# Attention with sorted blocks and a feed-forward layer on one core: query of batch 0 by turning products, weights in column halves, and a new written order

## The chip, the cores and the metric

The kernel runs on 1 core of one Trainium2 chip. The metric is the device time of one execution in microseconds (us). The core has five engines that each work through a queue of their own: TensorE (PE in the profile; its weight loads are PEld), VectorE (DVE), ScalarE (ACT), GpSimd (POOL) and SyncE (SP). PE writes to the accumulators (PSUM) only, and DVE and ACT bring results from there to the on-chip memory. Transfers run on 16 DMA engines. POOL issues the loads that turn float32 into bfloat16 on the way (queue q0 in the profile); SP issues the transposing transfers and the stores (q1).

## What is computed

Shapes: q, k and v are 4 batches x 8 heads x 768 tokens x 64, each head in 8 blocks of 96 tokens; sort_net is 4 x 8 x 8 x 8.

```python
for _ in range(5):                                   # sinkhorn on sort_net
    P = exp(P - max(P, -1)); P /= sum(P, -1) + 1e-9; P /= sum(P, -2) + 1e-9
k_sorted, v_sorted = P mixes the 8 blocks of k, of v  # einsum 'bhij,bhjcd->bhicd'
scores = q_b @ k_sb.T / 8                             # 96 x 96, one block with its own sorted block
attn = softmax(scores);  x = attn @ v_sb              # heads joined: 3072 tokens x 512
h = x @ w_in                                          # 512 -> 2048
g = max(h, 0) + alpha * min(h, 0)
out = g @ w_out                                       # 2048 -> 512, float32
```

## The kernel before, in words

**Work units.** A group g (0 to 31) is one block of one batch over all 8 heads; groups 0 to 7 are batch 0. `attention` makes for each group: scores (s1, 8 products into psS), their row maximum on DVE (tile nm or nf), the exponential on ACT, the weighted sum with v (PV, 8 products into psO), reciprocal `rec` and scaling `xq` on DVE, and the turn of xq into the feature-major tile xT. Batch 0 does not turn its probabilities: a second set of products with the roles exchanged (s2, 16 products, L765 and L756) gives the scores turned, with the maximum subtracted by products. Groups 0 to 15 turn xq by 4 products on PE (L823) and a copy; later groups by an SP transfer.

**Preparation of a batch.** `prep_q` (batch 0 only) brings q in feature-major order into QTz; q's DMA for batch 0 lands in the part of hT that is not yet used. `prep_k` mixes the blocks of k by products with BDK or BDM (matrices that `spread0` and `spread` make from the sinkhorn result) into KT. `conv_v` reorders v, and `prep_v` mixes it into VS. For batch 0 there are 6 units of q, 6 of k, 8 of v; each is some products and one copy out of PSUM (L400 is the helper that all copies share). Batches 1 to 3 have q loaded into QN and turned by SP (`turn_q`), k first spread into KSz by POOL (`conv_k`), v into VDz.

**Feed-forward.** `ffn1` makes, for one of 16 slices ft of 128 hidden features and one chunk of tokens, 4 products into psH (or psP), then ACT writes relu(-h) to t1 (L857) and DVE adds (1-alpha)*t1 to h and stores hT (L860). The chunks are groups (0,2), (2,4) of 192 tokens, then 7 chunks of 4 groups (384 tokens). `ffn2` makes a tile of 128 output tokens in four parts of 4 products each (part p uses ft 4p to 4p+3), copies it to outstg and stores it. The last tile, 23, comes in two halves of columns.

**What sets the order.** Every step is entered by `G.add` with the tiles it reads and writes; the steps are numbered in the order of these calls. `SEQ` is a written list of these numbers: each engine executes its steps in the order in which they stand there, and waits where a step's inputs are not ready. Nothing overtakes: a step that waits holds all later ones of its engine, and POOL's and SP's DMA issues stand in the same queues as their other work. A letter after a number picks the engine (p, a, d) where more are allowed; without it the first allowed one is meant, ACT for `EITHER`. `i15Y` means 15 filler products (L1017, 128 x 512, results not used) into an accumulator named by the letter. `burst` (L912) is a series of tiny products at the start. The planner in `_Graph.arrange` only gives each step a place in the waits; it does not reorder.

**Names used below.** hT<-in_q_dram is batch 0's q, VST<-in_v_dram is v, KS<-in_k_dram is k. VD (in hT) is the reordered v of batch 0. QTz, KT and VS are the prepared q, k and v. The four w_in loads and the two w_out loads are issued by POOL (L931, L936): w_in by 128 rows of 2048 columns each, w_out by halves of its 2048 rows. FFN1 waits for all four parts of w_in.

Of the kernel before, what the change touches and what calls it, by code (L numbers as in the profile page):

```python
# [7 lines left out]
AP = bass.AP  # L8
ACTF = mybir.ActivationFunctionType
# [18 lines left out]
BURST = 110  # L28
# [4 lines left out]
0 2 11 7 3 4 1 8 9 i15Y 22 42 28 14 43 44 45 46 19 47 18 48 5 49 50 51 15 39 52 53 54 6 55 56 57 25 58 29 59  # L33
23 60 61 12 62 63 64 132 65 66 37 31 67 89 68 83 32 69 81 13 70 84 87 71 91 10 88 85 i8Y 72 40 73 90 130 74 75
86 76 133 41 77 82 78 131 92 79 i2Y 134 80 93 138 102 94d i2Y 103 26 104 147 95 105 100 148 96d 98 i4Y 99 24
101d 38 35 111a 113 97d 17 107d i2Y 158 149 106a 108d 21 159 146 i2Y 114 118 115 116 135 160 119 144 109a 124
143 125d 117 150 110a i3Y 136 145 112a i2Y 122 141 120 161 121d 30 20 123 140 36 i3Y 128 126 129d 142 151 127
137 16 139 162 152 163 164 i3G 153 165 154 183 155 166 184 i1P 167 156 157 33 i2Y 185 168 34 169 192 186 195
170 198 193 171 204 174 194 205 201 187 202 196 206 203 199 188 200 219 197 207 216 27 189 213 220 237 217 221
214 190 218 228 191 215 225 238 208 226 222 209 223 227 239 229 210 246 234 224 240 211 247 230 231 212d 235  # L40
260 253 236 290 261 241 232 248 250 242 272 262 251 249 233 291 269 252 254 270 263 350 172 255 243 292 264
271 256 258 265 293 244 312d 278 311 273 279 259d 303 337 280 266 257 245d 284 338 267 281 300 285 294 268 339
299 286 282 310 402 283 313 295 301 296 401 340 287 274 302d 304 288 314 289 347 297 309 305 315 316 298d 319
306d 317 346 341 320 378 318 307 321 322 342 308 379 325 275 323 351 324 177 343 348 326 328 175 380 327 329
355 179 349d 344 331 330 276 352 176 345d 334 381 178 353d 372 332 335 333 382 356 336 360 383 357 389 363 384
373 361 364 354 362 390 365 387 366 388d 393 385 369 367 359 386d 391 368 358 418 392 428 419 370 403 374 429
371 445 420 395 431 396d 375 430 394d 397 376 434 449 452 432 435 377 404 421 448 453 398d 436 405 447 454 181
433 399 444 458 400d 464 437 459 455 465 450 456 406 460 180 479 466 457 482 446 451d 422 182 461 423 478 483
424 476 462 407 484 467 475 477 463 494 408 474 480 495 485 481 425 504 548 486 426d 496 487 509 506 438 507d
491 505 439 488 440 492 497 535 510 493 489 524 511 441 490 515 508 442 525 512 516 534 536 517 513 468 549  # L50
414 526 469 470 521 412 514 471 537d 518 417 522 527 472d 538 523 410 519 498 560 539 499 520 545 411 409 500
542 277 546 413 561 501 540 543 550 416 502 544 562 547 415 554 541d 557 570 551 555 571 563 558 556 572 574
552 596 559 578 573 575 597 528 607 579 605 529 581 598 427 606d 608 590 530 576 580 443 591 577 582 609 583
531 625 599 637 532 584 626 610 636 564 585 587 611 569 565 627 566 634 612 592 586 635d 567 613 588 628 638
589 614 593 568 615 553 616 639d 594 503 619 617 600 620 640 601 595 661 618 641 473 621 622 602 658 623 603
676 659 645 604d 662 677 643 663 642 624 678 644 629 667 630 631 664 668 660 703 669 665 670 704 666 673 671
533 173 691 674 705 675 692 672 688 713 632 685 706 689 633d 690 712 693 686 679 687 700 717 718 701 697 714
702 694 698 715 699 723 695 748 719d 720 696 724 716 738 721 749 739 732 750 647 725 648 733 740 722 649 753
680 646 754d 729 747 681 726 741 682 730 767 776 731 727 707 734 768 683 781 735 728 769 777 708 709 778 755
751 736d 758 756 770 812 802 757 759 787 760 752 710 761 803 780 764 762 788 846 763 765 804 657 766 789 779d  # L60
651 793 653 742 805 794 782 743 784 744 654 790 795 785 745 656 783 786 771 837 791 772 650 813 773 796 838
655 774 799 797 814 825 652 798 800 792 811 815 839 801 826 816d 847 822 853 819 823 840 849 872 824 820 806
848 817 821 827 711 818 873 831 807 834 808 832 828 833 835 874 836 850 854 829d 883 857 851d 882 866 855 875
852 858 856 841 859 880 900 684 881 842 860 901 884 861 863 843 910 746 885 867 862 864 887 902 865 908 886
844 888 909d 911 891 868 889 903 892 912 893 876 913 869 809 877 890 878 914 897 915 737 894 870 879 898 934
# [10 lines left out]
1147 1142 1138 1143 1144 1151 1148 1152 1139 1153 1149 1150 1157 1140d 1220 1158 1154 1141 1159 1181 1155 1156  # L76
# [234 lines left out]
def bass_sinkhorn_attn__then__act_prelu_kernel(  # L311
# [610 lines left out]
    for u in range(6):  # L922
        prep_q(u, -50, (BANK_H + BANK_O + BANK_S)[u])
# [136 lines left out]
```

## Time and profile before

| what | value |
|---|---|
| median of 3 runs | 237.89 us (237.42 to 238.29) |
| the profiled execution | 238.1 us, of which span 236.4 us |
| PE busy | 227.3 us (96% of the span), 2483 products |
| DVE, ACT, POOL busy | 167.4, 158.7, 99.0 us |
| granted TensorE clock | 1.0 in all 40 slices |
| moved by DMA | 31.36 MB, mean 133 GB/s |

The span runs from the first to the last instruction. The 1.7 us between span and time lie outside of what the profile shows. The duration of a product includes the time in which its result drains (about 0.17 us) beside the next one, so the start of one product to the start of the next is what it costs PE; a busy PE is not PE at its peak. In the timeline, a line is a start, a duration, the engine, the line of code, the operation, destination<-sources, shapes and a count of merged instructions.

### The profile page before, as it was taken

What the parts mean: (1) busy time and instruction counts of PE and PEld (TensorE: products, weight loads), DVE (VectorE), ACT (ScalarE), POOL (GpSimd) and SP (SyncE); (2) the same over time, 40 slices, a digit from 0 to 9 for tenths busy, and PEclk for the clock granted to TensorE, in tenths of its full rate; (3) what the DMA queues carried; (4) which work ended last, traced back from release to release, by engine and by line L of the source; (5) the groups of instructions that cost most, each with busy time, mean ns of one, the idle gap of its engine ahead of it and who ended that gap; (6) DMA issues with size and microseconds to landing.
All of it is one profiled execution on the core that took longest, in us unless ns stands there. A gap on an engine that the chain in (4) does not pass through costs nothing.

```text
span 236.4 us, 6202 instructions
## 1 busy us (share of the span) xinstructions
PE 227.3 (96%) x2483; PEld 141.6 (60%) x2513; DVE 167.4 (71%) x343; ACT 158.7 (67%) x429; POOL 99.0 (42%) x144
## 2 busy tenths in 40 slices
PE   7898989999999999999999999999999999999995
PEld 3455677777666756655656565556555555555553
DVE  4764789998899988776888777566777667554420
ACT  4579456688989898676767778777676783543332
POOL 7989507934679995308999534000000000000000
PEclk9999999999999999999999999999999999999999
DMA  5999999995697998998889967594445222310023
GB/s 96 212 207 214 169 219 197 179 190 120 115 181 137 85 210 137 185 183 179 147 133 113 167 70 150 131 145 104 94 137 131 63 50 50 137 42 2 0 101 124
DMA packets 71981, 31.36 MB, mean 133 GB/s; under 512 B 64512, under 2 KB 67344, under 8 KB 71952
## 3 DMA queue, kind: packets, MB, share of 16 engines
q0 software_dynamic: 23408, 13.63, 44.3%
q1 hardware_dynamic: 48544, 17.33, 36.2%
q8 instruction: 20, 0.33, 0.6%
q14 instruction: 9, 0.07, 0.1%
HBM read 27.28 MB, written 6.29 MB: 142 GB/s over the span
## 4 chain that ended last, share of the span: by engine, by line
PE 85%; DMA 5%; ACT 4%; DVE 2%; POOL 2%; issue 2%; POOLq 0%
PE psH L847 34%; PE psYP L886 30%; DMA VST<-in_v_dram 5%; PE psS L886 4%; PE psS L741 4%; PE psO L797 3%; PE psYP L698 2%; PE psYP L657 2%; ACT hT L400 2%; PE psS L756 2%; PE psS L765 1%; PE psO L823 1%; ACT VS L400 1%; POOL VDz L484 1%; DVE nm L750 1%
## 5 line engine op out<-in xcount | busy, mean ns | idle before, releaser
L860 DVE SCALAR_TENSOR_TENSOR hT<-t,omaT,psH 128x384 bf16<-128x384 f32 (+1 forms) x139 | 77.3, 570 | 35.6 <-ACT t L857 34.4
L847 PE MATMUL psH<-xT,w_in_bf 128*128 128x384 bf16 (+1 forms) x556 | 97.9, 310 | 0.5 <-DVE rec L805 0.5
L857 ACT ACTIVATE t<-psH 128x384 f32<-128x384 f32 (+1 forms) x139 | 62.6, 462 | 41.9 <-PE psH L847 39.1
L886 PE MATMUL psYP<-w_out_bf,hT 128*128 128x512 bf16 x308 | 78.6, 379 | 1.6 <-issue 0.2
L847 PEld LDWEIGHTS psH<-xT,w_in_bf 128*128 128x128 bf16 x556 | 49.1, 98 | 29.3 <-DVE hT L860 2.3
L886 PEld LDWEIGHTS psYP<-w_out_bf,hT 128*128 128x128 bf16 x336 | 31.4, 98 | 29.7 <-ACT outstg L400 0.2
L777 ACT ACTIVATE Esb<-psS,nf 96x96 bf16<-96x96 f32 x192 | 46.2, 344 | 4.0 <-DVE nf L750 4.0
L400 POOL COPY VDz<-VST 64x384 bf16<-64x384 bf16 x40 | 33.9, 847 | 20.0 <-PE psYP L698 9.8
L644 POOL COPY KSz<-KS 64x512 bf16<-64x512 bf16 x36 | 22.1, 615 | 18.2 <-DMA KS<-in_k_dram 9.2
L750 DVE TENSOR_REDUCE nf<-psS 96x8 f32<-96x768 f32 x24 | 22.8, 951 | 4.1 <-PE psS L741 3.6
L808 DVE TENSOR_TENSOR xq<-psO,rec 96x512 bf16<-96x512 f32 x31 | 21.3, 688 | 0.7
L429 POOL DMA_DIRECT2D QN<-in_q_dram x24 | 19.8, 858 | 0.3 <-POOL QN L489 0.3
L400 ACT ACTIVATE outstg<-psYP 128x512 f32<-128x512 f32 x18 | 10.8, 598 | 5.3 <-PE psYP L886 5.1
L1017 PE MATMUL psYP<-identb 128*128 128x512 bf16 x46 | 13.3, 420 | 0.7 <-ACT identb L400 0.7
L797 PEld LDWEIGHTS psO<-VS,ET 112*128 112x128 bf16 x248 | 11.0, 98 | 3.4 <-ACT ET L788 0.3
L741 PEld LDWEIGHTS psS<-KT,QTz 128*96 128x96 bf16 x192 | 11.5, 125 | 2.1 <-ACT Esb L777 0.2
L797 PE MATMUL psO<-VS,ET 112*128 112x65 bf16 x248 | 12.7, 194 | 0.0
L741 PE MATMUL psS<-KT,QTz 128*96 128x96 bf16 x192 | 12.6, 208 | 0.0
L400 DVE CAST VS<-psYP 112x512 bf16<-112x512 f32 x15 | 10.3, 689 | 3.0 <-PE psYP L703 2.1
L698 PEld LDWEIGHTS psYP<-BDV,VDz 128*128 128x128 bf16 x192 | 8.3, 98 | 3.1 <-DVE VS L400 0.3
L805 DVE RECIPROCAL rec<-psO 96x8 f32<-96x8 f32 x31 | 6.2, 201 | 5.3 <-PE psO L797 5.2
L698 PE MATMUL psYP<-BDV,VDz 128*128 128x64 bf16 x192 | 9.5, 193 | 0.0
(139 smaller groups left out, 201.5 us busy)
## 6 DMA issues: line engine op xcount, KB each, us to landing
out_dram<-outstg SPq DMA_DIRECT2D x23, 256.0 KB, 2.4
KS<-in_k_dram POOLq DMA_DIRECT2D x3, 768.0 KB, 7.7
QN<-in_q_dram POOLq DMA_DIRECT2D x24, 96.0 KB, 6.0
w_in_bf<-in_moe_w_in_dram POOLq DMA_DIRECT2D x4, 512.0 KB, 11.2
w_out_bf<-in_moe_w_out_dram POOLq DMA_DIRECT2D x2, 1024.0 KB, 23.3
VST<-in_v_dram POOLq DMA_DIRECT2D x4, 384.0 KB, 16.0
hT<-in_q_dram POOLq DMA_DIRECT2D x1, 768.0 KB, 7.0
VST<-in_v_dram POOLq DMA_DIRECT2D x1, 768.0 KB, 10.7
```

The lines of the kernel that those rows point to most:

```text
L400: return e.activation(o, i, ACTF.Copy) if e is nc.scalar else e.tensor_copy(o, i)
L644: G.add(POOL, lambda e, hp=hp: e.tensor_copy(AP(KSz, hp * 64 * 3072 + u % 3 * 1024 + hp * 64, [[3072, 64], [128, 8], [1, 64]]), AP(KS[n], ...
L698: inst = e.matmul(AP(t, off + dd * 64, [[row, 128], [1, 64]]), AP(VDz, (u % VSL * 8 + dd) * 128, [[VSL * 1024, 128], [1, 128]]), AP(BDV, b ...
L741: inst = e.matmul(o, AP(QTz[n], hp * 3072 + h4 * 768 + i * 96, [[6144, 128], [1, 96]]), AP(KT[n], (h4 * 8 + i) * bk, [[ld, 128], [64, 2], ...
L750: G.add(DVE, lambda e: e.tensor_reduce(AP(nx, 0, [[8, 96], [4, 2], [1, 4]]), AP(psX, 0, [[1024, 96], [512, 2], [96, 4], [1, 96]]), AxisLis ...
L777: inst = e.activation(AP(Esb[me], p * 128, [[1024, 96], [64, 2], [1, 48]]), AP(psX, (p // 4) * 512 + (p % 4) * 96, [[1024, 96], [48, 2], [ ...
L797: inst = e.matmul(AP(psZ, hp * 512 + h4 * 68, [[1024, 128], [1, 65]]), AP(ET[me] if far else ET[m], pos(h4, hp) * 96, [[800, nk], [1, 128] ...
L808: G.add(DVE, lambda e: e.tensor_tensor(out=AP(xq[me], 0, [[512, 96], [256, 2], [64, 4], [1, 64]]), in0=AP(psZ, 0, [[1024, 96], [512, 2], [ ...
L847: inst = e.matmul(AP(pt, poff, [[1024, 128], [1, n]]), AP(w_in_bf, kt * DFF + ft * 128, [[KT_TILES * DFF, 128], [1, 128]]), AP(xT, kt * XR ...
L857: G.add(ACT, lambda e: e.activation(AP(t1[tb], 0, [[384, 128], [1, n]]), AP(pt, poff, [[1024, 128], [1, n]]), ACTF.Relu, scale=-1.0), t_ac ...
L860: G.add(DVE, lambda e: e.scalar_tensor_tensor(out=AP(hT, ft * RING + tok % RING, [[FT_TILES * RING, 128], [1, n]]), in0=AP(t1[tb], 0, [[38 ...
L886: inst = e.matmul(AP(bank[0], bank[1], [[1024, 128], [1, n]]), AP(hT, ft * RING + tok % RING, [[FT_TILES * RING, 128], [1, 128]]), AP(w_ou ...
```

## The change

1. **q of batch 0.** Its DMA takes, for each of the 128 partitions, 6 tokens of each of the 8 heads (8 pieces of 384 numbers) instead of one piece of 3072. The 96 products of 64 columns become 48 turning products (128 partitions, 64 columns of weights, a moving identity of 128), 12 to a unit, with bfloat16 results in psS and psO. The copies out become 4 of 128 x 768 instead of 6 of 128 x 512.
2. **w_in.** Each of the four loads takes 2 blocks of 128 rows and 1024 columns. FFN1 of ft 0 to 7 waits for the two loads of the first column half, ft 8 to 15 for the two of the second.
3. **FFN1 of the two 192-token chunks in pairs.** Two slices ft share one accumulator bank and one relu of 384 numbers; the store step stays one per slice.
4. **Choice of engine.** BDM and BDV may be made on POOL; the scaling xq may be made on ACT, as 8 operations.
5. **The start burst** has 208 tiny products instead of 110.
6. **A new list.** POOL issues the first column half of w_in, then batch 1's k, then the second half, then w_out's first half, one head of batch 1's q, batch 1's v, seven more heads, and w_out's second half (before: all of w_in, w_out's first half, k, v, one head, w_out's second half, seven heads). Of the 8 reorderings of v of batch 0, ACT has 2, DVE 3 and POOL 3 (before: 5, 2, 1). The fillers are 42 (before 49).

```diff
-BURST = 110
+BURST = 208
...
-            G.add(POOL, lambda e: e.dma_start(AP(hT, 8192, [[HR, 128], [1, 3072]]), AP(q.tensor, 0, [[3072, 128], [1, 3072]])),
+            G.add(POOL, lambda e: e.dma_start(AP(hT, 8192, [[HR, 128], [384, 8], [1, 384]]),
+                                              AP(q.tensor, 0, [[384, 128], [S * D, 8], [1, 384]])),
...
     def prep_q(u, prio, bank):
-        G.add(PE, pairs(hT, 8192, u, identb, 0, 128, bank), 372, r=[("QS", 0), "identb"], w=keys, prio=prio)
-        o = AP(QTz[0], 8 * u, [[6144, 128], [96, 32], [48, 2], [1, 8]])
-        i = AP(t, off, [[row, 128], [2, 32], [1, 2], [64, 8]])
+        def f(e):
+            for x in range(6):
+                for hp in range(2):
+                    inst = e.matmul(AP(t, hp * 64 * 2048 + 2 * off + x * 128, [[2048, 64], [1, 128]]),
+                                    AP(hT, 8192 + (hp * 4 + u) * 384 + x * 64, [[HR, 128], [1, 64]]),
+                                    identb[:, :], is_transpose=True)
+        o = AP(QTz[0], u * S, [[6144, 128], [6, 128], [1, 6]])
+        i = AP(t, 2 * off, [[2048, 128], [1, 128], [128, 6]])
...
+        k = 2 if n == 192 else 1
...
-        op = G.add(PE, f, t_pe(*[(n, 128)] * 4), r=[("xT", g % 16) for g in range(ga, gb)] + [("w_in", kt) for kt in range(KT_TILES)],
+        op = G.add(PE, f, t_pe(*[(n, 128)] * (4 * k)), r=[("xT", g % 16) for g in range(ga, gb)] + [("w_in", ft // 8 * 2 + x) for x in range(2)],
...
-            AP(w_in_bf, p * DFF, [[KT_TILES * DFF, 128], [1, DFF]]),
+            AP(w_in_bf, p % 2 * 2 * DFF + p // 2 * 1024, [[KT_TILES * DFF, 128], [DFF, 2], [1, 1024]]),
```

The rest of the diff is the list and the choices of engine.

More of the change, by code (lines that the diff above doesn't have):

```diff
@@ L38 @@
[L38 to L42, printed above, removed]
@@ L440, in turn_q @@
             4500, r=[("QN", h) for h in range(H)] + [("turned", 8 * b - 8 + t)] * (b > 1),
-            w=[("QTzt", n, t)] + ([("Q0", u) for u in range(6)] if n == 0 and t == 0 else []),
+            w=[("QTzt", n, t)] + ([("Q0", u) for u in range(4)] if n == 0 and t == 0 else []),
             prio=prio, dma=(d_qt[t], 0))
@@ L852, in ffn1 @@
-        op = G.add(PE, f, t_pe(*[(n, 128)] * 4), r=[("xT", g % 16) for g in range(ga, gb)] + [("w_in", kt) for kt in range(KT_TILES)],
-              w=keys, prio=prio)
+            for x in range(k):
+                for kt in range(KT_TILES):
+                    inst = e.matmul(AP(pt, poff + x * n, [[1024, 128], [1, n]]),
+                                    AP(w_in_bf, kt * DFF + (ft + x) * 128, [[KT_TILES * DFF, 128], [1, 128]]),
+                                    AP(xT, kt * XR + tok % XR, [[KT_TILES * XR, 128], [1, n]]),
+                                    start=(kt == 0), stop=(kt == KT_TILES - 1))
@@ L860, in ffn1 @@
-        G.add(DVE, lambda e: e.scalar_tensor_tensor(
-            out=AP(hT, ft * RING + tok % RING, [[FT_TILES * RING, 128], [1, n]]),
-            in0=AP(t1[tb], 0, [[384, 128], [1, n]]), scalar=AP(omaT, ft, [[16, 128], [1, 1]]),
-            in1=AP(pt, poff, [[1024, 128], [1, n]]), op0=AluOpType.mult, op1=AluOpType.add),
-            t_dve(n) + 52, r=keys + [("t1", tb), "omaT"],
-            w=[("hT", ft, x % (RING // 64)) for x in range(tok // 64, (tok + n) // 64)], prio=prio)
+        G.add(ACT, lambda e: e.activation(AP(t1[tb], 0, [[384, 128], [1, k * n]]),
+                                          AP(pt, poff, [[1024, 128], [1, k * n]]), ACTF.Relu, scale=-1.0),
+              t_act(k * n), r=keys, w=[("t1", tb)], prio=prio)
@@ new lines, in ffn1 @@
+        for x in range(k):
+            G.add(DVE, lambda e, x=x: e.scalar_tensor_tensor(
+                out=AP(hT, (ft + x) * RING + tok % RING, [[FT_TILES * RING, 128], [1, n]]),
+                in0=AP(t1[tb], x * n, [[384, 128], [1, n]]), scalar=AP(omaT, ft + x, [[16, 128], [1, 1]]),
+                in1=AP(pt, poff + x * n, [[1024, 128], [1, n]]), op0=AluOpType.mult, op1=AluOpType.add),
+                t_dve(n) + 52, r=keys + [("t1", tb), "omaT"],
+                w=[("hT", ft + x, y % (RING // 64)) for y in range(tok // 64, (tok + n) // 64)], prio=prio)
```

128 lines of the change are left out of this document (74 added, 54 removed), and 18 rows, old and new, of the table SEQ.

## The prediction

> **What bounds the kernel now.** I read first two stages (each row: window, its length, busy time and count of PE, PEld, DVE, ACT, POOL, clock, DMA share, GB/s), cut where PE's timeline shows the first product of FFN1 (29.8), the first scores of batch 1 (58.9) and PE's end.
>
> ```profile
> 29.80:58.90 29.10, 27.95 (x431) 22.43 (x435) 26.94 (x68) 21.03 (x49) 14.36 (x21) 1.00 1.27 182
> 58.90:233.70 174.80, 172.98 (x1470) 103.58 (x1491) 121.66 (x212) 119.01 (x346) 60.41 (x82) 1.00 0.72 117
> ```
>
> From the first FFN1 product on, PE is busy 200.93 of 203.90 us: 1.15 us are idle before 58.9 and at most 1.82 us after it. The products that remain are the same after the change. So whatever is to be won lies in **when FFN1 starts**, plus about 1 us of gaps. The next question is what that start waits for. PE's timeline (start, duration, line, what):
>
> ```profile
> 8.38 0.44 PE L628 MATMUL psS<-identb,hT 64*64 64x64 bf16 x16 [0.69 <-DMA hT<-in_q_dram]
> ...
> 10.02 1.90 PE L1017 MATMUL psYP<-identb 128*128 128x512 bf16 x8
> ...
> 25.58 0.41 PE L797 MATMUL psYP<-VS,ET 112*128 112x65 bf16 x8
> ...
> 29.82 0.83 PE L847 MATMUL psH<-xT,w_in_bf 128*128 128x192 bf16 x8
> ```
>
> FFN1 starts 4.24 us after the first weighted sum (25.58), which needs all of VS. The timelines of ACT, DVE and POOL, and a stage row, show how VS comes about:
>
> ```profile
> 16.50 1.61 ACT L400 ACTIVATE hT<-VST 128x384 bf16<-128x384 bf16 x2 [0.24 <-DMA VST<-in_v_dram]
> ...
> 22.56 0.80 ACT L788 ACTIVATE ET<-psH 112x768 bf16<-112x768 f32 x1
> ...
> 24.75 0.68 ACT L400 ACTIVATE VS<-psO 112x512 bf16<-112x512 f32 x1 [0.73 <-PE psO L703]
> 16.50 0.99 DVE L400 COPY hT<-VST 128x384 bf16<-128x384 bf16 x2
> 17.39 0.95 DVE L750 TENSOR_REDUCE nm<-psH 96x8 bf16<-96x768 f32 x1
> 16.61 1.56 POOL L400 COPY hT<-VST 128x384 bf16<-128x384 bf16 x1 [0.97 <-DMA VST<-in_v_dram]
> 20.00:24.00 4.00, 3.54 (x57) 1.60 (x57) 2.25 (x3) 4.00 (x7) 3.97 (x6) 1.00 1.06 214
> ```
>
> v lands at 16.5; three engines begin to reorder it at once. From there to 25.58 are 9.1 us, and ACT fills them: 5 reorderings (0.81 each in the row), 5 copies of 0.68 and one exponential of 0.80 make 8.3 us. In 20 to 24 ACT is busy 4.00 of 4.00 us, DVE 2.25. So **two things** set FFN1's start: the landing of v, and ACT's share of the work behind it.
>
> **The change part by part.**
>
> *v's landing.* q, k and v of batch 0 are loaded one behind the other.
>
> ```profile
> hT<-in_q_dram POOLq DMA_DIRECT2D x1, 768.0 KB, 7.0
> DMA packets 287, 1.07 MB, mean 213 GB/s; under 512 B 31, under 2 KB 31, under 8 KB 285
> DMA packets 579, 0.61 MB, mean 203 GB/s; under 512 B 0, under 2 KB 578, under 8 KB 578
> DMA packets 227, 0.24 MB, mean 118 GB/s; under 512 B 3, under 2 KB 225, under 8 KB 227
> L425 POOL DMA_DIRECT2D hT<-in_q_dram x1 | 0.7, 692 | 0.8 <-POOLq L1045 0.8
> ```
>
> The DMA rows are the windows 18 to 23 (w_in, packets of 4 KB), 27 to 30 and 25 to 27 (w_out, 1 KB). q's new load has 1024 pieces of 768 B in bfloat16; the trace has no such packet. Bounds: the steady 1 KB window moves 203 where the 4 KB window moves 213 GB/s, by which q's 0.786 MB take 0.2 us longer; the first 2 us of w_out move 118, by which q takes 6.7 instead of 3.7 us, 3.0 longer. I take the steady row: in the slow window POOL was issuing heads of batch 1's q (24.75, below), beside q it issues only rows of one piece. The issue of 1024 pieces takes POOL 0.92 (w_out at 12.34, below) instead of 0.69 us: 0.2 more. v lands at 16.5 + 0.4 = **16.9**; for a gain I see no reason.
>
> The Trainium skill's page "DMA: Bandwidth & Descriptors", section Specifications, gives 512 B as the least transfer for line rate; by it 768 B would cost nothing and v land at 16.7. The trace agrees only in its steady window.
>
> *q's products and copies.* Nearest rows for the 48 turning products that replace 96:
>
> ```profile
> 27.01 0.34 PE L823 MATMUL psYP<-identb,xq 96*128 96x96 bf16 x4
> L823 PE MATMUL psO<-identb,xq x60: 203/205/217, 28.3 to 107.4; 96*128 96x96 bf16 x60
> L400 ACT ACTIVATE QTz<-psO 128x512 bf16<-128x512 f32 x2 | 1.2, 583 | 0.0
> ```
>
> Four turning products take 0.34, one 0.205, so they start 0.045 apart; with 128 columns for 96 that is 0.06, 2.9 us for all. Now q takes 1.65 (8.38 to 10.02). The 1.2 more lie where 1.90 us of fillers stand: nothing; without them they would delay k's mixing one for one. ACT copies 4 of 768 numbers (0.80, the exponential's row of that size) instead of 6 at 0.58: 0.3 less. One copy stands ahead of the sinkhorn's last exponential, and q is 0.4 late, so k's mixing and the first scores come 0.4 to 0.6 later (16.6 becomes 17.2). v covers that: DVE's first maximum stands behind a reordering that ends at 17.5.
>
> *The work behind v.* ACT now has 2 reorderings (1.6), 4 copies (2.7) and 2 exponentials (1.6): 5.9 instead of 8.3 us. DVE has 3 reorderings (1.5), 2 maxima (1.9) and 4 copies (2.7): 6.1. The two are even; but a copy waits for a product that waits for a bank, and the last copies on each follow that way, so I add 1.0 us of waits (before: 9.1 less 8.3). POOL has 3 reorderings: one at 1.56 beside a DVE copy, the others as in its other row:
>
> ```profile
> L400 POOL COPY VDz<-VST 64x384 bf16<-64x384 bf16 x40 | 33.9, 847 | 20.0 <-PE psYP L698 9.8
> L510 DVE TENSOR_REDUCE mkhV<-identf 128x8 f32<-128x128 f32 x1 | 0.3, 277 | 0.0
> ```
>
> The second is ready at 19.3 and the third, behind a memset, at 20.6; neither is last. First weighted sum: 16.9 + 6.1 + 1.0 = **24.0**.
>
> *From there to FFN1* the chain is the same (reciprocal, scaling, turn, copy), but the mask reduction above (0.28) now stands inside it on DVE, and `spread`'s 9 small products, which stood beside a wait, stand right ahead of FFN1 (about 0.3). 4.24 becomes 4.8; FFN1 at **28.8**, 1.0 earlier.
>
> *Behind FFN1's start.* One filler more: +0.2 (the eight above take 1.90). The pairs make 16 relus of 384 numbers of 32 relus of 192:
>
> ```profile
> L857 ACT ACTIVATE t<-psH 128x384 f32<-128x384 f32 x112 | 54.6, 495 | 39.0 <-PE psH L847 37.0 <-DVE hT L860 0.7
> L857 ACT ACTIVATE t<-psH 128x192 f32<-128x192 f32 x27 | 8.1, 328 | 2.9 <-PE psH L847 2.1 <-DVE hT L860 0.6
> ```
>
> ACT saves 2.6 us, but it is busy 21.03 of 29.1, so nothing by itself. DVE, at 26.94 of 29.1, is nearer to its limit; in the new list it has three fewer BDV, one BDM, three xT copies, one VDz copy and two copies of K and V in this stage, and one store copy more. So part of the 1.15 us of gaps goes. I take -0.5; bounds -1.15 (none left) and +0.7 (each first store of a pair waits 0.17 longer for its relu, in four places where PE has no spare bank). Behind 58.9 the products are the same and PE is full; two scalings on ACT lie where ACT is busy 119 of 174.8 us: nothing, bound +1.8, as much as is idle there now.
>
> *The burst* ends near 3 us; PE waits for q until 8.38: nothing.
>
> *The weights.* Issue (timeline of POOL) plus landing:
>
> ```profile
> 11.82 0.55 POOL L931 DMA_DIRECT2D w_in_bf<-in_moe_w_in_dram  x1
> 12.34 0.92 POOL L936 DMA_DIRECT2D w_out_bf<-in_moe_w_out_dram  x1
> 13.22 0.58 POOL L447 DMA_DIRECT2D KS<-in_k_dram  x1
> 19.46 0.91 POOL L936 DMA_DIRECT2D w_out_bf<-in_moe_w_out_dram  x1
> 24.75 2.47 POOL L429 DMA_DIRECT2D QN<-in_q_dram x3 [0.30 <-POOL QN L489]
> DMA to landing us min/median/max: 9.9/11.2/14.3
> DMA to landing us min/median/max: 20.3/20.3/20.3
> DMA to landing us min/median/max: 23.1/23.1/23.1
> DMA to landing us min/median/max: 26.2/26.2/26.2
> DMA to landing us min/median/max: 24.4/24.5/24.7
> ```
>
> The last w_in lands at 11.8 + 14.3 = 26.1, then w_out's first half at 32.6, k of batch 1 at 36.3, v (same size) at 40.0, one head and w_out's second half at 45.7, the last of seven heads at 26.4 + 24.4 = 50.8. Steps: 2.4 for each w_in load (16.5 to 26.1 for four), 6.5, 3.7, 3.7, 5.7, 5.1. New order from 16.9: first column half 21.7, k 25.4, second half 30.2, w_out 36.7, v 40.4, all heads and w_out's second half 51.2. PE needs them, by the products that the list puts ahead, at 28.8, 28.8 + 3.5, 28.8 + 9.1 and 28.8 + 22.8 = 51.6, plus gaps: covers of 7, 2, 1.2 and some 0.6 us. Nothing, but thin; the landings move with v, as PE's start does.
>
> **Sum:** -1.0 + 0.2 - 0.5 = -1.3 against the profiled 238.1 (span 236.4 and 1.7 around it). That run is 0.2 above the median of 237.89; so **236.6**.
>
> **The rivals.**
>
> *More comes of it.* With POOL at 0.85 throughout and half the waits FFN1 starts at 28.3, and the gaps shrink by 1.0: -1.5 + 0.2 - 1.0 = -2.3, 235.6. For it: DVE is lighter. Against: every queue still waits in its order.
>
> *POOL becomes the last.* If all three of its reorderings take 1.56, with a memset of 0.4 between, the third is ready at 16.9 + 5.1 = 22.0; a wait for its bank, product and copy put the weighted sum near 24.7, FFN1 at 29.5: -0.3 + 0.2 - 0.5 = -0.6, 237.3, no change that can be told. For it: the one such copy took 1.56. Against: 40 others took 0.85. The Trainium skill's "SBUF — State Buffer", section Who interferes with whom, says that a DVE copy in a two-port mode and a POOL instruction exclude each other for a whole instruction; by it the 1.56 are 0.85 and a wait for DVE's 0.99, and DVE's three copies, spread over the stage, can hit each of POOL's.
>
> *Slower: q's short pieces.* At 118 GB/s q takes 3.0 longer; with 0.2 for the issue v lands at 19.7, the weighted sum comes at 26.8, FFN1 at 31.6: +1.8 + 0.2 - 0.5 = +1.5, 239.4. It decides from v at 18.2 on, where the sum is zero. For it: w_out's first short pieces. Against: its later ones, at 203. A cover of the weights that breaks adds up to 1 and belongs here.
>
> *Turning products are slow.* At a whole L823 row each (0.205, nothing beside it) 48 take 9.8, to 18.5; the scores come 2 to 3 and the weighted sum some 2 later: +0.7 to +1, 238.8. The rows speak against it: four within 0.34, at clock 1.0. The Trainium skill's "TensorE: Matmul & The Clock Gate", section PE-mode transpose, gives about 0.275 in a kernel for 128x128, and says that such products do not keep the clock up; by it q would take 13.2 us.
>
> **How the numbers follow.** Forecast (235.9 to 237.1) 0.36; more 0.20; POOL last 0.19; short pieces 0.21; slow turning 0.04. A measurement of this kernel tells about 0.3%, 0.7 us. Faster 0.36 + 0.20 = 0.56; same 0.19; slower 0.25. The range reaches from the better end, with all gaps gone and an unseen 0.8 behind 58.9 (234.5), to the short pieces (239.3).
>
> **What would show it.** In the changed profile: v's reorderings start at 16.9 (from 18.2 on the slower rival decides); the first weighted sum at 24.0; FFN1 at 28.8; PE idle between FFN1 and batch 1's scores under 1.15; no PE wait on the weights; POOL's three reorderings at 0.85 or 1.56. What would make it wrong is a stall of PE that I priced at nothing, above all for w_out's second half, or a gap behind 58.9.

## The result, and the profile after

The changed kernel takes 240.62 us (median of 12 executions, 239.02 to 248.83), the kernel before in the same series 238.31 (237.42 to 238.77). The ratio is **1.0088** (95% interval 1.0069 to 1.0108): slower by 0.9%. I had forecast 236.6, range 234.5 to 239.3, and faster. The two highest executions, 247.51 and 248.83 at a mean clock of 0.979, are left out of the ratio. The profiled execution of the changed kernel took 239.51 us, span 237.4. Between span and time lie 2.0 to 2.1 us in every execution of the changed kernel, where the kernel before has 1.7: 0.3 us of the loss stand outside of what the profile shows, and their cause is open.

The two stages that the prediction began with, for the changed kernel (same columns; its PE ends at 234.7):

```profile
29.80:58.90 29.10, 28.91 (x444) 23.17 (x442) 26.78 (x62) 23.95 (x44) 18.37 (x27) 1.00 1.33 173
58.90:234.70 175.80, 173.38 (x1474) 102.62 (x1472) 120.68 (x211) 116.23 (x349) 60.02 (x83) 1.00 0.71 116
```

In the first stage PE now idles 0.19 us (before: 1.15), in the second 2.42. The early part, by PE's timeline, with two later lines:

```profile
8.87 0.53 PE L643 MATMUL psO<-identb,hT 128*64 128x128 bf16 x12
...
24.65 0.41 PE L808 MATMUL psYP<-VS,ET 112*128 112x65 bf16 x8 [0.26 <-DVE omaT L967]
...
29.14 0.83 PE L870 MATMUL psH<-xT,w_in_bf 128*128 128x192 bf16 x8
...
67.61 0.40 PE L808 MATMUL psO<-VS,ET 112*128 112x65 bf16 x8 [0.69 <-DMA ET<-Esb]
...
84.62 0.40 PE L808 MATMUL psO<-VS,ET 112*128 112x65 bf16 x8 [1.22 <-DMA ET<-Esb]
```

The first weighted sum comes 0.9 us earlier than before, FFN1 0.7, batch 1's first scores at 56.31 instead of 58.92. (1.1 of these 2.6 us are work that the new list does later: behind that point stand two FFN2 parts more, 0.865 each, and one FFN1 step less, 0.65.) So the kernel is 1.5 us ahead there, and loses that and 1.0 more. The waits of PE behind 56 us, as the profile sums them, hold one large entry that before has not (beside 0.3 us in front of an output tile at 131 us; before has one wait there, 0.5 us in front of an FFN1 step at 135 us, which is gone):

```profile
PE psO L808 <- DMA ET<-Esb: 1.9, 2, 1.2
```

ET are the softmax weights of a group, turned by an SP transfer; L808 is the weighted sum with v. A wait costs PE 0.17 us more than the idle time shown, because the last product's drain counts as busy: by the starts of the products PE loses 0.86, 0.30 and 1.38 us in front of the sums of groups 8, 11 and 12, and 0.44 at 131 us, 3.0 in all; less the wait that is gone, 0.6 by the same count, this is nearly the whole of the 2.5. Why are those transfers late? SP's queue in the changed kernel (start, duration, what):

```profile
44.93 6.15 SPq L439 DMA_TRANSPOSE QTz<-QN  x3
56.63 0.37 SPq L924 DMA_DIRECT2D out_dram<-outstg  x1
57.05 6.26 SPq L439 DMA_TRANSPOSE QTz<-QN  x2
63.36 1.29 SPq L793 DMA_TRANSPOSE ET<-Esb  x1
64.69 1.51 SPq L439 DMA_TRANSPOSE QTz<-QN  x1
66.24 1.30 SPq L793 DMA_TRANSPOSE ET<-Esb  x1
67.59 0.58 SPq L924 DMA_DIRECT2D out_dram<-outstg  x1
```

and its waits:

```profile
SPq L924 <- DVE outstg L401: 5.5, 1, 5.5
```

SP stands 5.5 us in front of the store of output tile 0, until DVE has copied the tile. Two turns of batch 1's q (t2, t3) have to wait behind it, although their data were there, and then take 6.26 us to issue (one of them 4.7 alone), while batch 2's v and the store are moving. Group 8's weights are ready at 60.16; their transfer is issued at 63.36. In the kernel before SP stands in front of the same store for 8.0 us, from 55.4 to 63.4, but group 8's transfer, whose weights are ready at 62.7, comes right behind it:

```profile
50.79 4.62 SPq L437 DMA_TRANSPOSE QTz<-QN  x3
63.38 0.37 SPq L900 DMA_DIRECT2D out_dram<-outstg  x1
63.80 1.68 SPq L782 DMA_TRANSPOSE ET<-Esb  x1
```

So the length of the wait does not tell its cost; what stands behind it does. For groups 10 to 12 it is another matter: there the transfers are issued at once and move slowly. Issue to landing of the weights' transfers issued from 55 to 85 us, five before and six after:

```profile
DMA to landing us min/median/max: 2.8/4.4/4.7
```

```profile
DMA to landing us min/median/max: 3.0/5.6/8.3
```

What they meet are batch 2's loads, by POOL's queue of the changed kernel:

```profile
55.75 0.58 POOL L465 DMA_DIRECT2D VST<-in_v_dram  x1
56.34 0.85 POOL L401 COPY VDz<-VST 64x384 bf16<-64x384 bf16 x1
63.30 2.86 POOL L401 COPY VDz<-VST 64x384 bf16<-64x384 bf16 x3 [6.12 <-PE psH L870]
66.24 0.29 POOL L615 TENSOR_TENSOR BDV<-mkhV,dsel 128x64 bf16<-128x64 f32 x1
66.59 0.83 POOL L401 COPY VDz<-VST 64x384 bf16<-64x384 bf16 x1
67.37 0.60 POOL L449 DMA_DIRECT2D KS<-in_k_dram  x1
```

The profile names a PE product for the 6.1 us; but the copy behind them is the first that reads batch 2's v, whose load landed at 63.1, and that is what POOL waited for. So k of batch 2 (768 KB) is issued at 67.4 (before: 59.7), and its eight q loads from 70.6 on (before: 77.8), right beside the weights of groups 10 to 12. From the trace, in us ("ready" is the end of the last exponential of the group):

| group | kernel | weights ready | issued | landed | first product |
|---|---|---|---|---|---|
| 8 | before | 62.70 | 63.80 | 68.18 | 69.17 |
| 8 | changed | 60.16 | 63.36 | 67.48 | 67.61 |
| 10 | before | 69.94 | 71.75 | 74.70 | 77.54 |
| 10 | changed | 68.40 | 68.43 | 76.75 | 77.01 |
| 12 | before | 79.82 | 79.84 | 84.53 | 87.13 |
| 12 | changed | 77.35 | 77.38 | 84.49 | 84.62 |

Where "first product" follows "landed" by 0.13, PE was waiting.

### The profile page after: what moved, and what is told of

Read it like the earlier page. It is cut to its first block, busy times and chain, and to the rows that moved or that the text cites. A ratio compares the mean times of both kernels' runs of the same rounds, so it can differ in the third digit from the quotient of the medians.

```text
span 237.4 us, 6314 instructions
## 1 busy us (share of the span) xinstructions
PE 228.5 (96%) x2556; PEld 142.2 (60%) x2556; DVE 169.2 (71%) x338; ACT 156.9 (66%) x424; POOL 102.8 (43%) x150
## 4 chain that ended last, share of the span: by engine, by line
PE 76%; ACT 8%; DMA 7%; DVE 6%; issue 1%; POOL 1%; SPq 0%; POOLq 0%; DVEq 0%
PE psH L870 29%; PE psYP L910 24%; DMA ET<-Esb 5%; PE psS L910 4%; ACT Esb L788 3%; PE psYP L1042 3%; PE psO L808 3%; PE psS L752 3%; DMA xT<-xq 2%; ACT t L880 2%; PE psYP L668 2%; ACT VDz L401 1%; PE psS L767 1%; PE psYP L709 1%; DVE hT L401 1%
## 5 line engine op out<-in xcount | busy, mean ns | idle before, releaser
L880 ACT ACTIVATE t<-psH 128x384 f32<-128x384 f32 x126 | 61.2, 494 | 48.4 <-PE psH L870 45.4
L910 PE MATMUL psYP<-w_out_bf,hT 128*128 128x512 bf16 x336 | 83.2, 379 | 0.3 <-DVE outstg L401 0.3
L870 PEld LDWEIGHTS psH<-xT,w_in_bf 128*128 128x128 bf16 x560 | 50.0, 98 | 29.0 <-DVE hT L884 1.8
L821 DVE TENSOR_TENSOR xq<-psO,rec 96x512 bf16<-96x512 f32 x29 | 19.8, 684 | 2.1 <-DMA xT<-xq 1.5
L808 PEld LDWEIGHTS psO<-VS,ET 112*128 112x128 bf16 x248 | 10.9, 98 | 6.5 <-ACT VS L401 1.7
L808 PE MATMUL psO<-VS,ET 112*128 112x65 bf16 x248 | 12.7, 194 | 2.0 <-DMA ET<-Esb 1.9
L1042 PE MATMUL psYP<-identb 128*128 128x512 bf16 x39 | 12.0, 429 | 0.4 <-ACT identb L401 0.2
L401 ACT ACTIVATE VS<-psYP 112x512 bf16<-112x512 f32 x13 | 8.9, 683 | 2.4 <-PE psYP L714 1.3
L401 ACT ACTIVATE outstg<-psYP 128x512 f32<-128x512 f32 x11 | 6.6, 599 | 5.8 <-PE psYP L910 5.8
L401 DVE CAST VS<-psYP 112x512 bf16<-112x512 f32 x13 | 8.9, 685 | 1.4 <-PE psYP L709 1.4
L910 PE MATMUL psS<-w_out_bf,hT 128*128 128x512 bf16 (+1 forms) x48 | 9.8, 344 | 0.0
```

Source lines behind the costliest of these rows:

```text
L401: return e.activation(o, i, ACTF.Copy) if e is nc.scalar else e.tensor_copy(o, i)
L808: inst = e.matmul(AP(psZ, hp * 512 + h4 * 68, [[1024, 128], [1, 65]]), AP(ET[me] if far else ET[m], pos(h4, hp) * 96, [[800, nk], [1, 128] ...
L821: return e.tensor_tensor(out=AP(xq[me], 0, [[512, 96], [256, 2], [64, 4], [1, 64]]), in0=AP(psZ, 0, [[1024, 96], [512, 2], [68, 4], [1, 64]]),
L870: inst = e.matmul(AP(pt, poff + x * n, [[1024, 128], [1, n]]), AP(w_in_bf, kt * DFF + (ft + x) * 128, [[KT_TILES * DFF, 128], [1, 128]]), ...
L880: G.add(ACT, lambda e: e.activation(AP(t1[tb], 0, [[384, 128], [1, k * n]]), AP(pt, poff, [[1024, 128], [1, k * n]]), ACTF.Relu, scale=-1. ...
L910: inst = e.matmul(AP(bank[0], bank[1], [[1024, 128], [1, n]]), AP(hT, ft * RING + tok % RING, [[FT_TILES * RING, 128], [1, 128]]), AP(w_ou ...
```

## The experiments

The theory after the result: the loss is made by late weights, partly by SP's order, partly by the place of the loads. The rivals: SP's order alone; TensorE's own order; and that the early part is itself slow.

**The turns ahead of the store.** In SP's queue of the changed kernel (174, 175, 176, 178: turns; 257, 341: stores; 385, 401, 431: weights of groups 8, 9, 10):

```diff
-174 257 175 176 385 178 401 341 431
+174 175 176 257 385 178 401 341 431
```

> The changed kernel, with SP's turns t2 and t3 of batch 1 put ahead of the store of output tile 0, so that they no longer stand between that store and the transposing DMA of group 8's weights. Theory (late weights): behind 56 us TensorE waits for the transposed weights of groups 8, 10, 11 and 12 (0.94, 0.1, 0.30 and 1.38 us in the changed kernel), the first because SP issues group 8's DMA 3.2 us after its weights are ready, the others because their DMAs take 7 to 8 us beside batch 2's loads. So group 8's DMA is issued at about 60.2 and the first wait goes, but the loads land when they did, and most of the 0.9 us comes back as a longer wait at groups 10 to 12: 240.0 to 240.6 us, against 240.6 for the changed kernel. Rival (only the queue): SP's order is the whole of it, the later waits go too, 238.5. Rival (full list): the loss lies in TensorE's own order, nothing moves, 240.6 with the waits in other places.

Measured: **236.12 us** (235.71 to 236.61), ratio to before 0.9904 (0.9876 to 0.9931): 4.5 us below the changed kernel's 240.62 and 2.3 faster than before. The rival that SP's order is the whole of it was right, and even it expected too little. SP's queue, and PE from 56.3 to 91 in this kernel and then in the changed one:

```profile
45.78 9.55 SPq L439 DMA_TRANSPOSE QTz<-QN  x5
56.00 0.37 SPq L924 DMA_DIRECT2D out_dram<-outstg  x1
59.54 1.42 SPq L793 DMA_TRANSPOSE ET<-Esb  x1
61.00 2.02 SPq L439 DMA_TRANSPOSE QTz<-QN  x1
63.15 1.22 SPq L793 DMA_TRANSPOSE ET<-Esb  x1
64.41 0.58 SPq L924 DMA_DIRECT2D out_dram<-outstg  x1
```

```profile
56.30:91.00 34.70, 34.34 (x371) 21.86 (x375) 29.25 (x51) 30.84 (x98) 26.00 (x35) 1.00 1.35 166
```

```profile
56.30:91.00 34.70, 32.55 (x359) 20.25 (x355) 27.50 (x47) 29.64 (x95) 24.51 (x33) 1.00 1.26 158
```

The turns use the time in which SP had stood still, group 8's weights go out 0.02 us after they are ready, and PE is idle for 0.36 us where it was for 2.15. I had expected the loads' waits to remain. They do not, because all that follows comes earlier: v lands at 61.7 instead of 63.1, the second store (67.59 in the changed kernel) is out of the way at 64.4, k is issued at 66.2 and lands at 73.2. The transfers of groups 10 to 12 still take 6.5, 6.9 and 5.5 us, but land just in time: products start 1.2, 0.14 and 0.16 us behind the landings, and PE loses 0.06 us at most.

**k of batch 2 earlier.** POOL's queue of the changed kernel (365, 366: v; 367: k; the others reorderings and small ones):

```diff
-365 168p 326 366 357 411 413 408 171p 409 367 410
+365 168p 326 366 357 367 411 413 408 171p 409 410
```

> The changed kernel, with the load of batch 2's k (768 KB) put on POOL ahead of the five reorderings that wait for batch 2's v, right behind the second v load: issued at about 57 in place of 67.4. Theory (late weights): it then moves beside v and not beside batch 2's q, so the transposing DMAs of groups 10 to 12 land 3 to 5 us after their issue, not 7 to 8, and the waits of 0.1, 0.30 and 1.38 us go; group 8's may grow by up to 1 us, as k now moves when its DMA is issued. 239.0 to 239.6 us, against 240.6. Rival (only the queue): the lateness is of SP's order, the waits stay, 240.6. Rival (q loads): the eight q loads alone are enough to hold the DMAs, latencies stay at 6 us and more, 240.3.

Measured: 242.23 us, ratio 1.0159 (1.0127 to 1.0191): no gain, 1.6 us above the changed kernel's 240.62 and level with its second series (242.11, below). The transfers of groups 10 to 12 do come down, to 2.8, 5.2 and 4.4 us, as the theory said. But now the two turns behind the store run beside k, take 11.6 and 10.3 us, and PE waits for one of them:

```profile
PE psS L752 <- DMA QTz<-QN: 4.0, 1, 4.0
```

**Three moves.** v of batch 2 earlier on POOL, k behind it, and the turns as above:

```diff
 POOL
-279 287 280 285 322 314 353 365 168p 326 366 357 411 413 408 171p 409 367 410
+279 287 365 366 280 285 322 314 353 168p 326 357 367 411 413 408 171p 409 410
 SP
-174 257 175 176 385
+174 175 176 257 385
```

> The changed kernel with three moves: both v loads of batch 2 some 9 us earlier on POOL (at about 44 to 46), k of batch 2 right behind the first copies that follow (about 55 to 57), and SP's turns t2 and t3 of batch 1 ahead of the store of output tile 0. Nothing that TensorE, ACT or VectorE do is touched. Theory (late weights): all four waits go, 2.5 us in all, 238.1 us, and the gain of the early part shows, at or just below the kernel before (238.3). Rival (full list): TensorE waits for the next late thing instead, 240 or more. Rival (w_out): the v loads hold back w_out's second half, which lands at 50.2 now and is first used at 53.2, and a wait of 1 to 2 us appears there: 239.5.

Measured: 240.12 us (12 executions), ratio 1.0054 (1.0032 to 1.0077): 4.0 us slower than the turns alone. All weights land with a cover of about 1 us or more; the lateness has moved to the turns, two of which now take 12.5 and 12.1 us behind w_out's second half and v, and to w_out:

```profile
PE psS L752 <- DMA QTz<-QN: 3.0, 2, 2.3
PE psYP L910 <- DMA w_out_bf<-in_moe_w_out_dram: 0.5, 1, 0.5
```

So it is not "loads early" that helps. Each place tried for them collides with something; the turns in SP's idle time do not.

**The loads late, in the kernel before** (403: k; 410 to 417: q):

```diff
-403 445 449 448 447 444 479 446 478 475 474 504 509 505 535 508 534 414 412 417 410 411 413 416 415
+445 449 448 447 444 479 446 403 478 414 475 412 417 474 410 411 504 413 416 415 509 505 535 508 534
```

> The kernel before, with batch 2's k load moved on POOL from 59.7 us to about 70, and its eight q loads put between the reorderings that follow, as the changed kernel has them; nothing else is touched, and nothing of the early part. Theory (late weights): the transposing DMAs of groups 10 to 12, which take 2.8 to 4.7 us here, take 7 to 8 beside these loads; their slack is 2.6 to 2.8 us, so TensorE waits 1.5 to 3 us in all at 77 to 88 us: 239.8 to 241.3 us against 238.3, the loss of the change without the change. Rival (full list, or the early part): the loads' place does not matter, 238.3.

Measured: 254.5 us, ratio 1.064 (1.0585 to 1.0695); the profiled execution took 257.36. This did not test what it was made for: the first q load must wait until q of batch 1 is turned, at 80.6, and it held POOL's reorderings of v behind it. The wait is in front of the products with v:

```profile
PE psYP L698 <- POOL VDz L400: 13.8, 3, 10.4
```

It shows the same mechanism at a larger size, a waiting transfer at the head of a queue. On the loads' place it says only that the one transfer of weights that met k took 8.4 us.

**Group 8's weights behind three turns, in the kernel before** (377: store; 421, 437: weights of groups 8, 9; 181, 180, 182: turns):

```diff
-377 421 181 437 180 182 467
+377 181 180 182 421 437 467
```

> The kernel before, with SP's transposing DMA of group 8's weights put behind the turns t4, t3 and t5 of batch 1 (it stood ahead of them): the changed kernel's place of that DMA, without any other part of the change. Theory (SP's queue): the DMA is issued at about 68 in place of 63.8, as three issues of 1.3 to 1.5 us stand ahead of it, and lands at 71 to 72.5; the weighted sum of group 8 begins at 69.2 and would wait 2 to 3.3 us; the turns come earlier, which nobody waits for: 240.4 to 241.7 us against 238.4. Rival (something else in the list): the order on SP does not cost time by itself, 238.4.

Measured: 244.41 us, ratio 1.026 (1.0207 to 1.0314), more than the 2 to 3.3 us expected. The wait is where it should be (three turns stand ahead of group 8's weights here, two and the store in the changed kernel; the weights of group 9 also move behind all three):

```profile
72.67 0.42 PE L797 MATMUL psO<-VS,ET 112*128 112x65 bf16 x8 [3.70 <-DMA ET<-Esb]
```

The order of one queue, with nothing else of the change, costs more than the change did. That the loss (6.2 us; by the two profiles' spans 241.6 less 236.4, 5.2) is larger than the wait has a reason of its own, told in the last section.

**The store behind.** The changed kernel's SP queue, the turns left in place:

```diff
-174 257 175 176 385 178 401 341 431
+174 175 176 385 178 401 257 341 431
```

> The changed kernel, with the store of output tile 0 put behind the transposing DMA of group 9's weights on SP; the turns t2 and t3 stay where they are, so they are issued as soon as t1 is, at about 51 to 54, and group 8's DMA when its weights are ready. Theory (head of the queue): what cost 4.5 us in the changed kernel is that SP sat 5.5 us in front of the store, waiting for DVE's copy, with the turns and group 8's DMA behind it; with the store out of the way 236.1 us, as with the turns ahead of it. Rival (bytes): it is the store's 256 KB beside the v loads that slow the transposing DMAs; moved to 63 us it would collide with those of groups 8 and 9 instead, a wait of 1 us or more, 237.2 to 238.5.

Measured: 237.20 us (10 executions), ratio 0.9947 (0.9927 to 0.9968). 3.4 of the 4.5 us are back: it was the wait at the head of the queue. The other 1.1 us are only in part the rival's: both stores are now issued at 64.5 and landed by 67.6, ahead of k, and groups 8 and 9 don't wait. Up to 69 us this profile runs 0.06 us behind that with the turns ahead. Then it loses 0.3 us ahead of an FFN1 step at 70.6, 0.55 at group 12's weights and 0.25 ahead of products with v at 83.4. The largest is this wait:

```profile
PE psO L808 <- DMA ET<-Esb: 0.4, 1, 0.4
```

**The order of the loads**, on the kernel with the turns ahead (134: k of batch 1; 126, 127: w_in's first column half):

```diff
-126 127 24 134 128
+134 126 127 24 128
```

> The kernel of e1_turns_first (236.12 us), with batch 1's k put back ahead of the first column half of w_in on POOL; the rest is as there. The question is what the new order of the loads is worth. Theory (cover): the first column half lands at 22.4 us in the changed kernel and FFN1 starts at 29.1; behind k it lands at about 26.5, still 2.6 us ahead, and k comes earlier than it is needed: 236.1 us, no PE wait on w_in. Rival (the order makes the gain): FFN1's first products wait for w_in, 1 us or more, 237.1 or above.

Measured: 236.43 us, ratio 0.9908 (0.9873 to 0.9943), no wait on w_in, whose first half lands at 25.9, 3.2 us ahead of FFN1. The column half ahead of k is worth nothing that can be told by itself.

**q by turning products alone, on the kernel before.** The first part of the change's diff, and the list without steps 89 to 92.

> The kernel before with the first part of the change alone: q's DMA in 8 pieces of 384 numbers for each partition, 48 turning products, 4 copies of 768 numbers; the list is that of before, without the steps of the two units that fall away. Theory (the list makes the early gain): v lands within 0.4 us of 16.5, ACT saves 0.3 us of copies, q's products end earlier but v and ACT's reorderings of it set the first weighted sum, which stays at 25.6: 238.0 to 238.6 us. Rival (q makes the early gain): the first scores come 0.5 us or more earlier and carry the rest along, FFN1 at 29.2 or before, 237.0 to 237.6. Rival (short pieces): v lands 1 us or more later, 239 or above.

Measured: 238.43 us (10 executions), ratio 1.0000 (0.9985 to 1.0016): nothing, with v landing at 16.0. In the profile the first weighted sum comes at 26.37, not at 25.6 as I expected, and FFN1 at 30.62. Whether that is of the edit one profile can't tell: the three profiles with the early part of the kernel before unchanged (before and the two experiments on its later part) have v at 16.5, 16.6 and 17.1 and FFN1 at 29.82, 29.98 and 30.89.

**Who reorders v.** Three kernels move pieces of batch 0's v. On the kernel with the turns ahead, two from POOL to ACT:

```diff
-POOL 105 102 109   ACT 103a 106a             DVE 104d 107d 108d
+POOL 105           ACT 103a 102a 109a 106a   DVE 104d 107d 108d
```

> The kernel of e1_turns_first (236.12 us), with two of POOL's three reorderings of batch 0's v put on ACT, behind its first: ACT has 4, DVE 3, POOL 1. The question is what made the early part faster. Theory (ACT's share): ACT's 2 more pieces of 0.81 to 0.88 us stand ahead of its 4 copies of VS, the first weighted sum comes 1.0 to 1.7 us later than 24.65 and FFN1 as much later than 29.1: 237.1 to 237.8 us. Rival (the last reordering): the third POOL piece at 20.7, or DVE's last at 22.1, sets the weighted sum; then ACT's pieces end earlier than those and the time stays or falls, 235.8 to 236.3.

Measured: 236.32 us, ratio 0.9901 (0.9863 to 0.9939), FFN1 at 29.35. Then one more from DVE to ACT, as the kernel before has it:

```diff
-POOL 105 102 109   ACT 103a 106a                  DVE 104d 107d 108d
+POOL 105           ACT 103a 102a 109a 106a 107a   DVE 104d 108d
```

> The kernel of e1_turns_first (236.12 us), with batch 0's v reordered by the engines of the kernel before: five of the eight pieces on ACT, two on DVE, one on POOL; that is one piece more on ACT than in e8_reorder_on_act, and DVE's first one gone. Theory (ACT's share, as in the prediction): ACT has 2.5 us more between v's landing and the first weighted sum than in e1_turns_first, of which its idle 1.2 us there cover half; the sum and FFN1 come 1.0 to 1.5 us later, 237.1 to 237.6 us. Rival (order of products): as in the two kernels before this one (0.2 us by two pieces here, nothing on the kernel before) who reorders v does not matter, 236.1 to 236.6.

Measured: 237.45 us, ratio 0.9965 (0.9927 to 1.0004): 1.3 us slower than with two pieces on ACT (236.12), 1.1 slower than with four. Outside of the span both kernels have 1.7 us again, not 2.0, so by spans (medians 234.1, 234.6 and 235.75) the differences are 0.5 and 1.6. FFN1, in the kernels with two, four and five pieces there:

```profile
28.51 0.83 PE L870 MATMUL psH<-xT,w_in_bf 128*128 128x192 bf16 x8
```

```profile
29.35 0.83 PE L870 MATMUL psH<-xT,w_in_bf 128*128 128x192 bf16 x8
```

```profile
29.71 0.83 PE L870 MATMUL psH<-xT,w_in_bf 128*128 128x192 bf16 x8
```

The first line can't be laid beside the other two as it stands: in its execution DVE's first piece of v took 0.52 us, in the other two 1.1 and 1.5 (last section). With two pieces on ACT and such a slow first piece FFN1 started at 29.14 (the changed kernel's first profile) and 29.11 (batch 1's k ahead). Beside these, four pieces on ACT cost 0.2 us and five 0.6; beside the profile with k ahead, five lose another 0.4 at the weights of groups 11 and 12 and 0.3 ahead of products with v.

And on the kernel before, three pieces away from ACT:

```diff
-POOL 113             ACT 111a 106a 109a 110a 112a   DVE 107d 108d
+POOL 113 109p 112p   ACT 111a 106a                  DVE 107d 108d 110d
```

> The kernel before, with three of ACT's five reorderings of batch 0's v moved: u=4 to VectorE behind the first maximum, u=3 and u=6 to POOL behind u=7, ahead of its issues of w_out's second half and q's heads (1.7 us later by this). Theory (ACT's share): ACT, which fills 8.3 of the 9.1 us from v's landing to the first weighted sum, loses 2.4 us; the sum begins 0.8 to 1.6 us earlier than 25.58 and FFN1 than 29.82: 236.8 to 237.5 us. Rival (chain through products and banks): what remains is set by the products' order and the accumulators, 238.0 to 238.4.

Measured: 238.37 us (10 executions), ratio 1.0012 (0.9992 to 1.0032), FFN1 at 30.40 with v landing at 17.3: nothing in the time. ACT is freed, and waits for PE instead:

```profile
23.19 0.68 ACT L400 ACTIVATE VS<-psO 112x512 bf16<-112x512 f32 x1 [1.25 <-PE psO L703]
...
25.33 0.68 ACT L400 ACTIVATE VS<-psO 112x512 bf16<-112x512 f32 x1 [1.39 <-PE psO L703]
```

So ACT's share costs something within the new list, less than the rows of ACT say, and is worth nothing in time within the old one. What holds the old list's products there I have not settled.

**The changed kernel again.**

> The changed kernel once more, for a second profile. Theory (late weights): the waits on the transposed weights of groups 8 and 10 to 12 come back at the same places, 2 to 4 us in all, with group 8's DMA issued 3 us or more after its weights are ready; 240 to 241 us. Rival (chance): the waits of the first profile were of that one execution, and lie elsewhere or are under 1 us in all.

Measured: four executions of 239.70 (the profiled one), 241.75, 242.47 and 243.97 us, median 242.11, ratio 1.0194 (1.0148 to 1.0240). The first series had 1.0088, so the size of the loss is known only as about 1 to 2%.

```profile
28.52 0.83 PE L870 MATMUL psH<-xT,w_in_bf 128*128 128x192 bf16 x8
```

```profile
PE psO L808 <- DMA ET<-Esb: 2.9, 3, 1.4
```

The waits are at groups 8, 10 and 12. This execution and that with the turns ahead start FFN1 within 0.01 us of each other, and group 8's weights are ready at 59.53 and 59.52; then the transfer is issued at 63.03 in the one and at 59.54 in the other. At group 8's first product they are 1.4 us apart (0.4 of it ahead of scores that wait for a turn), at group 12's 3.86, and from there to the end nothing is added (spans 237.6 and 233.8). That is the price of the order of SP's queue.

## Why the prediction was wrong

- **The step that failed** is "Behind 58.9 the products are the same and PE is full; ... nothing, bound +1.8". The products are the same, but I took PE's fullness there for a property of the stage. It was a cover of 1 to 2.8 us for each group's weights, and the change spends it: PE comes earlier, SP's transfers do not. I had followed POOL's queue load by load and never laid the new list's SP queue beside the old one, though the turns, the store and the weights all stand in it. The bound was too small as well: it took the idle time of the kernel before for all that could be lost, but the waits come to 3.0 us in one profile, and the other lost 3.86 against the better order.
- **The last sentence**, that a gap behind 58.9 would make it wrong, named the place; but it had no price and no chance in the sum. A row for SP's queue would have given one: group 8's cover of 1.0 us before, against a store that waits and two turns put between it and group 8's transfer.
- **The time around the span** (1.7) was taken over without a word. It is 2.0 to 2.1 in the changed kernel: 0.3 us more, a term that the sum does not have.
- **v's landing** (16.9): 16.3 in the changed kernel's first profile, 16.3 to 17.0 in the other five with the same early part. Right, but the spread of one early part from execution to execution (0.7, and 16.5 to 17.1 before) is larger than the 0.4 that was priced. The short pieces of q were no loss: q landed 7.2 to 7.9 us after its issue (before: 7.0).
- **Turning products** (0.06 each): 12 of them end after 0.53 us, at clock 1.0, which is 0.03 each, half of what I took; ACT's copies of 768 take 0.81 to 0.83 (0.80). Nothing hung on it, and q alone gives nothing, as I had it.
- **First weighted sum** (24.0) and **FFN1** (28.8): 24.65 and 29.14 in the first profile, 24.02 and 28.51 with the turns ahead, 24.03 and 28.52 in the changed kernel's second. Right within 0.7. How much of it is ACT's share is another matter: five pieces on ACT cost 0.6 us in front of FFN1, like beside like, not the 1.0 to 1.5 that I expected of them. What makes the rest of the early gain, of the many moves in the list, was not taken apart.
- **POOL's three reorderings** (0.85 or 1.56): 0.84, 1.06 and 0.83 in the first profile, 1.09, 1.05 and 1.96 in the second. The slow third one held nothing up; FFN1 came earlier in that profile. POOL was not the last.
- **The gaps** before 58.9 (-0.5): -0.96, near the bound of none left.
- **The weights** (21.7, 25.4, 30.2, 36.7, 40.4, 51.2): 22.4, 26.4, 31.0, 36.5, 41.1 and 50.2, and no wait on any. Right.
- **The early sum** (-1.3): the kernel with the turns ahead, which is the change without the failed step, has -2.3. By its profile FFN1 starts 1.3 us earlier (1.0 forecast), the way from there to the end is 1.3 shorter (0.3 forecast), and 0.3 come on top outside the span. My rival "more comes of it" (235.6) would have been the nearest, but in part by luck: it had 0.8 for the way behind FFN1's start, and nothing outside the span.

## What to carry to other kernels

When a list or an order is changed, lay each in-order queue that issues transfers beside its old self, and ask for every waiting entry what stands behind it and how much cover that has; a store that waits for its data belongs behind the transfers that are ready. A full engine shows that its covers hold today, not that they are large: before pricing an earlier start, read the slack of each transfer that does not move with it. Moving one load cures one collision and makes the next, so try the order of the small transfers first.

## What the runs showed of the hardware

**A long wait costs more than its length.** With k earlier, PE waits 4.05 us, and afterwards the granted clock (behind the engines' columns) is halved; the same after the 3.70 us with group 8's weights behind the turns:

```profile
67.00:70.00 3.00, 2.11 (x20) 1.63 (x21) 1.22 (x2) 0.68 (x1) 1.51 (x2) 0.50 1.18 240
70.00:72.00 2.00, 2.00 (x7) 0.73 (x6) 0.87 (x2) 1.52 (x7) 1.84 (x3) 0.50 0.91 233
...
76.00:80.00 4.00, 4.00 (x52) 2.76 (x50) 3.57 (x8) 3.70 (x12) 3.96 (x6) 1.00 0.65 50
```

```profile
74.00:76.00 2.00, 2.00 (x13) 0.96 (x12) 1.19 (x3) 1.11 (x2) 0.85 (x1) 0.50 0.13 23
...
78.00:80.00 2.00, 2.00 (x26) 1.30 (x25) 1.83 (x5) 2.00 (x10) 1.73 (x3) 1.00 0.00 0
```

The clock stood at 0.5 from 66.60 to 73.42 in the first, 6.8 us that begin 2.7 us into the wait, and from 73.26 to 76.67 in the second, 3.4 us that begin 0.6 behind the end of the wait. Of the 6.8, PE worked in 5.5. So work worth about 2.8 and 1.7 us of full clock was lost on top of the waits. Waits up to 1.4 us, as in the changed kernel's two profiles, and of 2.3 us in that of the three moves, left it at 1.0. The profile with the loads late has the shortest wait that was followed by half clock: 3.16 us, up to 127.35, and then 3.4 us at 0.5 from 127.70 on. So in these runs 2.7 us without work were enough, and 2.3 were not. The four executions of the changed kernel's second series go with this: 239.70 us at a mean clock of 1.0, 241.75 and 242.47 at 0.993, 243.97 at 0.986; that a longer wait halved the clock there too is argued, as they have no profile. The Trainium skill's page "TensorE: Matmul & The Clock Gate", section What's actually happening, has an idle window of about 3.4 us halve the rate, on windows that run freely. The traces agree in the lengths (3.4 us, and twice that) and in that the halving keeps no fixed distance from the wait; but a window wholly without work is not needed, as the 3.4 us ahead of each of these three halvings still held 0.3 to 0.7 us of PE's work.

**Transposing transfers and loads.** A transfer of weights takes 2.8 to 2.9 us from issue to landing alone, up to 9.4 beside POOL's loads (group 10 in the changed kernel's second profile), and turns up to 12.5 behind w_out's second half and v. The issue itself holds SP: 1.2 to 1.3 us alone, but for one turn 4.7 and 5.1 in the changed kernel's two profiles, 7.7 with k earlier and 7.9 with the three moves, while v, k or w_out were moving. Why it does was not tested.

**A copy beside POOL.** With the changed kernel's early part DVE's first piece of v took 0.52 to 0.54 us in five profiles and 1.81 in one, the changed kernel's first, with POOL's load issues and copies beside it:

```profile
16.52 1.81 DVE L401 COPY hT<-VST 128x384 bf16<-128x384 bf16 x1
17.11 1.96 POOL L401 COPY hT<-VST 128x384 bf16<-128x384 bf16 x2
```

It ended at 18.33, 0.38 us behind POOL's first piece (17.95). The three other kernels with a slow first piece on DVE (1.1 to 1.5 us: batch 1's k ahead, four and five pieces on ACT) have the same 0.37 to 0.38 us between these ends. FFN1 came 0.6 us later for it (29.14 and 29.11, against 28.29 to 28.54). What decides which of the two happens is open: v's landing does not, as it was at 16.30 in the slow one and at 16.34 in one of the quick ones.
